# A recurrent attention, a tanh network and an 8-expert layer on one core: order of the first loads, weight conversion through PSUM, a seventh place for weights

## The chip, the cores and the metric

The kernel runs on one core of a Trainium2 chip. The time is that of one execution on the device in microseconds, from three runs of the kernel before: 834.49, 833.47 and 834.39, median 834.39. One more execution was profiled; it took 832.75 us, with a span of 831.2 us from its first to its last instruction. All rows below come from that one.

## The reference, cut to what matters

```python
# r, k, v: [4, 8, 768, 48]; w, u: [8, 48]
def _attn_ref(r, k, v, w, u):
    state = zeros(B, H, D, D)
    for t in range(S):
        kt, vt, rt = k[:, :, t], v[:, :, t], r[:, :, t]
        cur = einsum('bhd,bhe->bhde', u[None] * kt, vt)
        y[:, :, t] = einsum('bhd,bhde->bhe', rt, state + cur)
        state = w[None, :, :, None] * state + einsum('bhd,bhe->bhde', kt, vt)

def _moe_ref(x, w_in, w_out):          # x: [3072, 384], w_in: [384, 2048], w_out: [2048, 384]
    h = x @ w_in
    return (h - np.tanh(h)) @ w_out

def _moe2_ref(x, expert_emb, tau, w1, w2):   # 8 experts, w1: [8, 384, 1024], w2: [8, 1024, 384]
    logits = normalised(x) @ normalised(expert_emb).T / tau
    expert_idx = argmax(logits); gate_w = softmax(logits)[expert_idx]
    out[token] = gate_w * (relu(x @ w1[e]) @ w2[e])      # e = expert_idx of the token

reference = _moe2_ref(_moe_ref(_attn_ref(...)), ...)
```

The arguments `w_in` and `w_out` of the second stage reach the kernel as 64-bit floats. They are read as 64-bit integers, and the kernel makes 32-bit floats of them by shifts and masks of the two 32-bit halves.

## The kernel before, in words

The sequence is cut into 24 tiles of 128 tokens (4 batches by 6 chunks), and three tiles make a block of 384 tokens. There are eight blocks. Every product of matrices is done with numbers split into a high part (type float32r) and a low part, the rest that the high part leaves, with three matmuls for each product (high by high, high by low, low by high).

**Attention of a tile** (class `Att`, L312). `decay_r` and `decay_k` (L324, L327) multiply the transposed r and k of the tile by tables of powers of w. `bonus` (L335, L336) forms r*k*u and `sums` (L340) adds it up over a head, `diagonal` (L348 on ScalarE with eight activations, or L350 on GpSimd with two instructions) makes diagonal matrices of the sums. `scores` (L361) is a TensorE product, `causal` (L366) copies the scores above the diagonal over the diagonal matrix, `values` (L391) multiplies by v and, after the first chunk, by the state, `result` (L396 on ScalarE, L397 on VectorE) writes the high and the low part of xt. `decayed` (L331) and `state_product` (L405), `state_add` (L414, L416, L419) carry the state on.

**Weights.** w_in and w_out come in 16 chunks of 128 x 768 numbers (chunk m: w_in for even m, w_out for odd m), in the order `order` (L1006). A chunk is loaded (L220, L225) into one of six places (`STAGE`, L208), of which two are tiles of their own and four are also the last quarters of the converted weights. `convert` (L228) makes floats of it, in place, with three VectorE instructions over 768 elements: L240 and L243 write `bits`, a tile in SBUF, and L246 writes the place. `split` (L252) then writes the high part on ScalarE (L253) and the low part on GpSimd (L254). A place is free for a later chunk once its chunk is split and, for w_out, transposed for the logits (`Logits`, L256). Logits: the product of w_out with the normalised expert embedding (`embedding_norms`, `embedding_rows`, `embedding_columns`, L1044 to L1060) is put into eight more columns of w_out (L285, L286), so that the second product of the network gives the router's logits as well.

**The network.** For a block, step f of 16 computes 128 hidden columns: `ffn1` (L469, nine matmuls into a PSUM tile ph), `squares` (L516, L517 on ScalarE), `small_tanh` (L525 and L526 on VectorE, L527 and L529 on ScalarE, then glo on VectorE, L532), and, two or three steps later, `ffn2` (L480, nine matmuls into three sums that stay in PSUM). Up to two instructions of a conversion are put between L526 and glo (L530, L531). All PSUM tiles share eight banks (L96).

**The order.** The part from L137 to L1141 is written by hand: within it each engine keeps the program's order (`manual_schedule`, L138). It issues the first loads (L1083 to L1091), the attention of tiles 0, 1 and 2 (block 0), and the first three conversions, in turns. Instructions that come later in the program may be put between those by the planner, which orders all the rest by a model of the time. Then comes a loop (L1194) of 22 steps: six of block 0 and sixteen of block 1, in which the attention of tiles 3, 4 and 5 (`attention_stage`, begun at the steps in `START`, L85) and the other conversions (at the steps in `CONV`, L86) are spread out. After it the other blocks run, each with the attention of the next one, and then the experts, with weights loaded anew. SP issues nearly all loads and stores, one after the other; a load whose buffer isn't free holds back those behind it.

`tc.issue_after(x)` brackets instructions that are to be issued after x; in the kernel before it is used with x on the same engine as the instructions inside it (L710, L746, L824, L1313).

## Time and profile before

| | |
|---|---|
| median of three runs | 834.39 us |
| the profiled execution | 832.75 us |
| its span | 831.2 us |
| TensorE (PE) busy | 773.0 us, 93% of the span |
| VectorE (DVE) busy | 525.6 us, 63% |
| ScalarE (ACT) busy | 440.8 us, 53% |
| GpSimd (POOL) busy | 309.1 us, 37% |
| moved by DMA | 89.69 MB, 108 GB/s over the span |

Shares over the whole span are a mean of stages that differ, so the first 160 us, in which the attention of the first tiles and the conversion of the weights take place, are to be read by themselves: with the busy time of each engine in a stretch, then with the waits of the engine that is due to be the bound, and then with the single instructions of the engine that it waits for. The last number of a waiting row is the longest single wait; "PEclk" is the mean clock that TensorE was granted in a stretch, as a share of 2.4 GHz.

### The profile page before, as it was taken

The numbers are of one execution on the slowest core, as the hardware profiler recorded it, in microseconds if no ns is written. First come the engines' busy times: TensorE is split into PE (matmuls) and PEld (weight loads), VectorE is DVE, ScalarE is ACT, GpSimd is POOL, SyncE is SP. The second block draws the span as 40 slices with busy tenths as digits, with TensorE's granted clock in tenths as the row PEclk, the third lists the DMA queues.
The fourth block names the chain that finished last, engine by engine and source line by source line (L and its number), as shares of the span: only waits on it lengthen the run. The fifth ranks groups of instructions, "written<-read, shape, count | busy, mean of one in ns | idle before, by whom it ended". The sixth has DMA issues, their size and how long they took to land. (4 is left out here: it accounts for less than half of the span.)

```text
span 831.2 us, 15313 instructions
## 1 busy us (share of the span) xinstructions
PE 773.0 (93%) x5835; PEld 726.2 (87%) x5835; DVE 525.6 (63%) x1048; ACT 440.8 (53%) x1007; POOL 309.1 (37%) x312
## 2 busy tenths in 40 slices
PE   6567979999999999999999999999989999999992
PEld 3456968897999999999999999999979999999992
DVE  8999698577786676676676684656554344454510
ACT  1256647555656656656655756777343435454421
POOL 7674254047363173173173250131431214331111
PEclk8578989999999999999999999999999999999996
DMA  8851721024323123123123201050552335544300
GB/s 285 279 162 41 261 71 54 24 84 121 115 69 112 54 85 112 56 82 112 53 85 112 77 8 58 30 181 20 160 165 90 135 113 189 188 132 163 122 28 29
DMA packets 41445, 89.69 MB, mean 108 GB/s; under 512 B 9328, under 2 KB 21024, under 8 KB 40338
## 3 DMA queue, kind: packets, MB, share of 16 engines
q1 hardware_dynamic: 37042, 79.10, 29.2%
q0 software_dynamic: 4320, 9.51, 3.5%
q8 instruction: 48, 0.79, 0.4%
q14 instruction: 35, 0.29, 0.1%
HBM read 69.82 MB, written 19.47 MB: 107 GB/s over the span
## 5 line engine op out<-in xcount | busy, mean ns | idle before, releaser
L469 PE MATMUL ph<-xt,wq 128*128 128x384 f32 (+2 forms) x1712 | 346.6, 345 | 2.6 <-DVE am L366 2.6
L469 PEld LDWEIGHTS ph<-xt,wq 128*128 128x128 f32 x1712 | 307.7, 192 | 7.9 <-DVE am L366 2.7
L480 PE MATMUL acc<-wq,ghi 128*128 128x392 f32 (+2 forms) x1120 | 291.2, 344 | 1.7 <-DVE wq L286 1.7
L480 PEld LDWEIGHTS acc<-wq,ghi 128*128 128x128 f32 (+1 forms) x1120 | 201.0, 188 | 7.4 <-DVE wq L286 2.0
L480 PE MATMUL acc<-wq,glo 128*128 128x392 f32 (+2 forms) x560 | 186.6, 341 | 5.5 <-DVE glo L532 5.5
L480 PEld LDWEIGHTS acc<-wq,glo 128*128 128x128 f32 (+1 forms) x560 | 104.6, 187 | 6.5 <-DVE glo L532 5.8
L516 ACT ACTIVATE z<-ph 128x384 f32<-128x384 f32 x128 | 62.5, 488 | 85.1 <-PE ph L469 84.8
L525 DVE TENSOR_TENSOR ph<-ph,z 128x384 f32<-128x384 f32 x128 | 71.8, 561 | 42.1 <-ACT z L516 41.7
L532 DVE TENSOR_TENSOR glo<-ph,ghi 128x384 fp32r<-128x384 f32 x128 | 70.9, 554 | 43.1 <-ACT ghi L527 42.2
L527 ACT ACTIVATE ghi<-ph 128x384 fp32r<-128x384 f32 x128 | 62.7, 490 | 53.6 <-DVE ph L526 49.2
L701 POOL DMA_INDIRECT out_dram<-ob,gts x27 | 28.7, 1064 | 154.6 <-ACT ob L779 149.1
L517 ACT ACTIVATE q<-z,sb_t 128x384 f32<-128x384 f32 x128 | 78.8, 615 | 3.3
L526 DVE SCALAR_TENSOR_TENSOR ph<-q,ph 128x384 f32<-128x384 f32 x128 | 71.8, 561 | 12.8 <-ACT q L517 4.5
L546 DVE SCALAR_TENSOR_TENSOR glo<-ph,ghi 128x384 fp32r<-128x384 f32 (+2 forms) x56 | 31.5, 563 | 74.1 <-ACT ghi L545 74.1
L529 ACT ACTIVATE mk<-z,lz_t 128x384 bf16<-128x384 f32 x128 | 77.0, 601 | 0.0
L545 ACT ACTIVATE ghi<-ph 128x384 fp32r<-128x384 f32 (+2 forms) x56 | 27.7, 496 | 72.7 <-PE ph L469 72.7
L748 DVE TENSOR_TENSOR wq<-eraw,wq 128x768 fp32r<-128x768 f32 x60 | 55.4, 960 | 16.9 <-ACT wq L747 15.8
L747 ACT ACTIVATE wq<-eraw 128x768 fp32r<-128x768 f32 x64 | 50.5, 837 | 11.5 <-DMA eraw<-in_moe_w_dram 11.5
L335 POOL TENSOR_TENSOR rk<-rkv 128x384 f32<-128x384 f32 x21 | 22.2, 1056 | 89.2 <-ACT xr L566 43.9
L350 POOL TENSOR_TENSOR am<-ident,cd 128x512 f32<-128x512 f32 x42 | 45.0, 1092 | 13.1 <-DVE cd L340 13.0
L254 POOL TENSOR_TENSOR wq<-wraw,wq 128x768 fp32r<-128x768 f32 x16 | 30.6, 1915 | 43.3 <-ACT wq L253 43.3
L327 POOL TENSOR_TENSOR tt<-tt,tab_k 112x512 f32<-112x512 f32 x20 | 36.3, 1815 | 18.9 <-DMA tt<-in_cols_dram 18.9
(272 smaller groups left out, 887.9 us busy)
## 6 DMA issues: line engine op xcount, KB each, us to landing
eraw<-in_moe_w_dram SPq DMA_DIRECT2D x32, 768.0 KB, 4.9
rkv<-in_rows_dram SPq DMA_DIRECT2D x22, 640.0 KB, 5.4
tt<-in_cols_dram SPq DMA_DIRECT2D x22, 448.0 KB, 4.0
xd<-xt SPq DMA_DIRECT2D x8, 1152.0 KB, 6.0
wraw<-in_moe_w_in_dram SPq DMA_DIRECT2D x8, 768.0 KB, 7.4
wraw<-in_moe_w_out_dram SPq DMA_DIRECT2D x8, 768.0 KB, 7.1
xs<-xr SPq DMA_DIRECT2D x21, 192.0 KB, 2.2
first<-in_rows_dram SPq DMA_DIRECT2D x1, 640.0 KB
```

The costliest lines, as they stand in the source:

```text
L350: nc.gpsimd.tensor_tensor(out=a, in0=ident[:, None, :].to_broadcast([P, HP, P]), in1=self.cd[:, :, g:g + 1].to_broadcast([P, HP, P]), op=A ...
L469: nc.tensor.matmul(out=ph, lhsT=lhs[a][:, kk, :], rhs=rhs(b, kk), start=(kk == 0 and p == 0), stop=(kk == nk - 1 and p == 2))
L480: mm = nc.tensor.matmul(out=acc[t], lhsT=g[a][:, t * P:t * P + m], rhs=rhs(b, i), start=(i == span[0] and p == 0), stop=(i == span[1] - 1 ...
L516: nc.scalar.activation(out=z, in_=ph, func=AF.Square)
L517: nc.scalar.activation(out=q, in_=z, func=AF.Square, scale=SS, bias=sb_t)
L525: nc.vector.tensor_tensor(out=ph, in0=ph, in1=z, op=ALU.mult)
L526: nc.vector.scalar_tensor_tensor(out=ph, in0=q, scalar=KC, in1=ph, op0=ALU.add, op1=ALU.mult)
L527: nc.scalar.activation(out=ghi, in_=ph, func=AF.Copy)
L529: nc.scalar.activation(out=mk, in_=z, func=AF.Relu, bias=lz_t, accum_out=zx[:, step:step + 1])
L532: nc.vector.tensor_tensor(out=glo, in0=ph, in1=ghi.bitcast(F32), op=ALU.subtract)
L747: nc.scalar.activation(out=hi[c][:, a], in_=t[:, a], func=AF.Copy)
L748: engs[s % len(engs)].tensor_tensor(out=lo[c][:, a], in0=t[:, a], in1=hi[c][:, a].bitcast(F32), op=ALU.subtract)
```

## The change

Twelve edits, most of them before the loop of 22 steps:

- `convert` works on a chunk in two parts (w_in: two of 384 elements; w_out: 512 and 256). The first two instructions of each part write a PSUM tile from the pool of eight banks instead of `bits` in SBUF, and the third reads it. There are six instructions instead of three for a chunk, and three of them, not two, may stand ahead of glo.
- The space of `bits`, of one of two buffers of `mk` and one of two of `t` gives a seventh place for weights (tag `stg6`), and `STAGE` uses it. `part` and other users of the six places keep theirs.
- First loads: the embedding and tau come ahead of tiles 1 and 2, only three chunks of weights are loaded at the start (`load_next(3)`), the fourth comes after the rows of tile 3, the next after those of tile 4, and tile 5's load comes last of all.
- Hand order: the bonus of tiles 1 and 2 moves from VectorE to GpSimd; the diagonals of tiles 0, 1 and 2 move from GpSimd to ScalarE; tile 2's decays and scores come ahead of the results of tiles 0 and 1; the first conversion, split half by half, comes ahead of tile 2's result, and the second and the third come behind it. The state products of tiles 1 and 0 and the embedding's columns are now in this part.
- `START` and `CONV`: tile 5 begins one step later, and the fourth and the fifth conversion are one step later.
- `store_x` is put in an `issue_after` of the ScalarE instruction L527 of the latest step.

```diff
-    START = (0, 1, 1)
-    CONV = (0, 1, 3, 5, 6, 7, 8, 9, 11, 12, 13, 15, 18)
+    START = (0, 1, 2)
+    CONV = (1, 2, 3, 5, 6, 7, 8, 9, 11, 12, 13, 15, 18)
-    STAGE = (0, 1, 2, 3, 0, 1, 2, 3, 2, 3, 4, 5, 1, 4, 1, 1)
+    STAGE = (0, 1, 2, 3, 6, 0, 1, 2, 3, 6, 4, 5, 1, 6, 1, 6)
-        x = work.tile([P, 2 * DM], I32, name="bits", bufs=1)
+            cuts = [[x.rearrange("p (k f d) -> p f k d", k=NK, d=P)[:, i] for x in (lo, hi)] for i in range(2)]
...
+            cuts = [[x[:, i:j] for x in (lo, hi)] for i, j in ((0, 512), (512, 2 * DM))]
...
+            for l, h in cuts:
+                x = ps.tile([P, 512], I32, tag="p", name="bits")
+                x = x[:, :TOK].rearrange("p (k d) -> p k d", d=P) if win_chunk else x[:, :l.shape[1]]
+                nc.vector.tensor_scalar(out=x, in0=h, scalar1=3, scalar2=0x3FFFFFFF,
+                                        op0=ALU.logical_shift_left, op1=ALU.bitwise_and)
+                yield
+                nc.vector.scalar_tensor_tensor(out=x, in0=l, scalar=29, in1=x,
+                                               op0=ALU.logical_shift_right, op1=ALU.bitwise_or)
+                yield
+                nc.vector.scalar_tensor_tensor(out=l, in0=h, scalar=-0x40000000, in1=x,
+                                               op0=ALU.bitwise_and, op1=ALU.bitwise_or)
+                yield
...
-    def split(f, dst_hi, dst_lo, eng=None):
+    def split(f, dst_hi, dst_lo, eng=None, i=slice(None)):
...
     def store_x(j, xt):
-        nc.sync.dma_start(...)
+        with tc.issue_after(mark["z"]):
+            nc.sync.dma_start(...)
...
-        nc.scalar.activation(out=ghi, in_=ph, func=AF.Copy)
-        mk = work.tile([P, TOK], BF16, name="mk")
+        mark["z"] = nc.scalar.activation(out=ghi, in_=ph, func=AF.Copy).ins
+        mk = work.tile([P, TOK], BF16, name="mk", bufs=1)
...
-        next(between, None)
-        next(between, None)
+        for _ in range(3):
+            next(between, None)
...
-    def load_next():
+    def load_next(n=NF):
-            if before and order[before[-1]] not in done or STAGE[s] > 3 and 5 not in finished:
+            if before and order[before[-1]] not in done or STAGE[s] in (4, 5) and 5 not in finished:
...
+    nc.sync.dma_start(out=en, in_=emb)
+    nc.sync.dma_start(out=tau_t, in_=tau.to_broadcast([P, 1]))
     load_rkv(1)
     load_rkv(2)
-    nc.sync.dma_start(out=en, in_=emb)
-    nc.sync.dma_start(out=tau_t, in_=tau.to_broadcast([P, 1]))
-    load_next()
-    load_rkv(5)
+    load_next(3)
...
     a[0].decay_k(nc.vector)
-    decay_rows()
     a[0].sums()
-    a[0].diagonal()
+    a[0].diagonal(True)
     a[0].scores(range(HP))
+    embedding_norms()
+    a[1].bonus(nc.gpsimd)
     a[1].decay_r(nc.vector)
     a[1].decay_k(nc.vector)
-    a[1].bonus(nc.vector)
     a[1].sums()
+    decay_rows()
+    a[1].diagonal(True)
     a[1].scores(range(HP))
-    a[1].diagonal()
     a[0].causal()
     a[0].values()
-    a[2].bonus(nc.vector)
+    a[2].bonus(nc.gpsimd)
+    a[2].decay_r(nc.vector)
+    a[2].decay_k(nc.vector)
     a[2].sums()
+    a[2].scores(range(HP))
+    a[2].diagonal(True)
     a[1].causal()
     a[1].values()
-    a[2].diagonal()
     a[0].result()
-    a[2].decay_r(nc.vector)
-    a[2].decay_k(nc.vector)
-    a[2].scores(range(HP))
+    a[1].decayed()
+    a[1].state_product()
+    load_rkv(3)
+    load_next(4)
+    a[2].causal()
+    a[2].values()
     a[1].result()
-    embedding_norms()
-    a[1].decayed()
+    ops = convert_next()
+    for i in range(2):
+        for _ in range(3):
+            next(ops)
+        split(*ready[0], i=i)
+    done.add(0)
     a[0].decayed()
+    a[0].state_product()
+    load_rkv(4)
+    load_next()
+    load_rkv(5)
+    a[2].result()
+    embedding_rows()
+    embedding_columns()
     convert_now()
-    a[2].causal()
-    convert_now()
-    split(*ready[0])
-    done.add(0)
-    a[2].values()
-    embedding_rows()
-    a[1].state()
-    a[2].result()
-    load_rkv(3)
-    load_next()
     split(*ready[1])
+    a[2].decayed()
+    a[1].state_add()
     convert_now()
     split(*ready[2])
...
         if i == 0:
-            a[0].state_product()
-            a[2].decayed()
-            load_rkv(4)
-            embedding_columns()
             routing_table()
```

The lines left out give `t` and `mk` one buffer wherever they are made, and name the places.

## Rows read from the trace of the kernel before

**Rows 1.** The page, part 1: busy us (share of the span) xinstructions.

```profile
PE 773.0 (93%) x5835; PEld 726.2 (87%) x5835; DVE 525.6 (63%) x1048; ACT 440.8 (53%) x1007; POOL 309.1 (37%) x312
```

**Rows 2.** Busy time by stretch; columns: start:end, length, engines (instructions), clock, DMA share, GB/s.

```profile
7.70:39.60 31.90, 17.07 (x189) 12.70 (x190) 30.20 (x38) 4.48 (x10) 20.98 (x16) 0.63 0.90 303
39.60:80.00 40.40, 27.08 (x198) 23.23 (x196) 40.21 (x50) 22.86 (x60) 24.08 (x16) 0.75 0.33 105
80.00:110.00 30.00, 30.00 (x316) 27.90 (x316) 22.05 (x36) 19.09 (x47) 10.00 (x6) 0.98 0.67 228
110.00:130.00 20.00, 13.58 (x66) 11.62 (x65) 19.85 (x22) 9.31 (x22) 13.08 (x10) 0.83 0.13 40
```

**Rows 3.** Waits of TensorE, 30 to 130 us: for whom, us, times, longest.

```profile
PE pt L267 <- DVE wraw L246: 8.2, 1, 8.2
PE acc L480 <- DVE glo L532: 5.5, 1, 5.5
PE ps_en L1059 <- DVE en L1054: 4.4, 1, 4.4
PE ph L469 <- DVE am L366: 2.6, 1, 2.6
PE acc L480 <- DVE wq L286: 1.7, 1, 1.7
```

**Rows 4.** Groups of VectorE's instructions, 10 to 82 us: busy us, mean ns.

```profile
L243 DVE SCALAR_TENSOR_TENSOR bits<-wraw,bits 128x768 int32<-128x768 int32 x8 | 15.5, 1936 | 0.0
L246 DVE SCALAR_TENSOR_TENSOR wraw<-wraw,bits 128x768 int32<-128x768 int32 x8 | 9.1, 1135 | 0.1
L240 DVE TENSOR_SCALAR bits<-wraw 128x768 int32<-128x768 int32 x8 | 9.0, 1125 | 0.0
...
L324 DVE TENSOR_TENSOR tt<-tt,tab_r 112x512 f32<-112x512 f32 x4 | 6.9, 1727 | 0.0
...
L336 DVE TENSOR_TENSOR rk<-rk,u_bc 128x384 f32<-128x384 f32 x2 | 1.8, 919 | 0.1
...
L335 DVE TENSOR_TENSOR rk<-first 128x384 f32<-128x384 f32 x1 | 1.4, 1397 | 0.0
...
L335 DVE TENSOR_TENSOR rk<-rkv 128x384 f32<-128x384 f32 x1 | 0.5, 546 | 0.0
```

**Rows 5.** Single lines, to 200 or 300 us: shortest/median/longest ns, first and last start.

```profile
L240 DVE TENSOR_SCALAR bits<-wraw x16: 537/560/2156, 23.7 to 147.2; 128x768 int32<-128x768 int32 x16
L243 DVE SCALAR_TENSOR_TENSOR bits<-wraw,bits x16: 943/1258/7008, 24.3 to 147.8; 128x768 int32<-128x768 int32 x16
L246 DVE SCALAR_TENSOR_TENSOR wraw<-wraw,bits x16: 943/960/2621, 27.5 to 149.2; 128x768 int32<-128x768 int32 x16
L525 DVE TENSOR_TENSOR ph<-ph,z x29: 548/560/567, 49.8 to 196.0; 128x384 f32<-128x384 f32 x29
L366 DVE COPY_PREDICATED am<-cmask,pa x28: 715/727/749, 15.6 to 299.0; 128x512 f32<-128x512 uint8 x28
```

**Rows 6.** Timeline, 111 to 118 us: start us, us, engine, line, operation.

```profile
111.59 7.01 DVE L243 SCALAR_TENSOR_TENSOR bits<-wraw,bits 128x768 int32<-128x768 int32 x1
112.12 1.86 POOL L254 TENSOR_TENSOR wq<-wraw,wq 128x768 fp32r<-128x768 f32 x1
...
116.80 0.99 POOL L336 TENSOR_TENSOR rk<-rk,u_bc 128x384 f32<-128x384 f32 x1
```

**Rows 7.** Timeline at 15 to 56 us, single rows.

```profile
15.75 2.04 POOL L350 TENSOR_TENSOR am<-ident,cd 128x512 f32<-128x512 f32 x2 [1.08 <-DVE cd L340]
...
33.03 0.39 SPq L220 DMA_DIRECT2D wraw<-in_moe_w_in_dram  x1
...
38.62 0.56 DVE L397 TENSOR_TENSOR xt<-py,xt 128x384 fp32r<-128x384 f32 x1
...
55.64 2.44 ACT L348 ACTIVATE am<-ident,cd 128x128 f32<-128x128 f32 x8
```

**Rows 8.** The page, part 6, DMA issues: xcount, KB each, median us to landing.

```profile
wraw<-in_moe_w_out_dram SPq DMA_DIRECT2D x8, 768.0 KB, 7.1
```

More of the change, by code (lines that the diff above doesn't have):

```diff
@@ L206, in rwkv__then__tanh_ffn__then__top1_moe_kernel @@
     CW = 2 * P
-    STAGE = (0, 1, 2, 3, 0, 1, 2, 3, 2, 3, 4, 5, 1, 4, 1, 1)
+    STAGE = (0, 1, 2, 3, 6, 0, 1, 2, 3, 6, 4, 5, 1, 6, 1, 6)
     def stage(i, shape, dt, name):
-        return work.tile(shape, dt, name=name, tag=f"stg{i}" if i < 2 else f"wq{i - 2}3", bufs=1)
+        return work.tile(shape, dt, name=name, tag=f"wq{i - 2}3" if 1 < i < 6 else f"stg{i}", bufs=1)
     def raw(s):
@@ L452, in store_x @@
     def store_x(j, xt):
-        nc.sync.dma_start(out=blocks(xd, j * TOK).rearrange("(p a) d -> p (a d)", p=P),
-                          in_=xt.rearrange("p k i t -> p (k i t)").bitcast(F32))
+        with tc.issue_after(mark["z"]):
+            nc.sync.dma_start(out=blocks(xd, j * TOK).rearrange("(p a) d -> p (a d)", p=P),
+                              in_=xt.rearrange("p k i t -> p (k i t)").bitcast(F32))
     def attention(j):
@@ L486, in tanh_parts @@
         q = work.tile([P, TOK], F32, name="q")
-        t = work.tile([P, TOK], F32, name="t")
-        mk = work.tile([P, TOK], BF16, name="mk")
+        t = work.tile([P, TOK], F32, name="t", bufs=1)
+        mk = work.tile([P, TOK], BF16, name="mk", bufs=1)
         nc.scalar.activation(out=z, in_=ph, func=AF.Square)
@@ L511, in any_tanh @@
         return halves(tanh_join(ph, tanh_parts(ph)))
+    mark = {}
     def squares(ph):
@@ L526, in small_tanh @@
         nc.vector.scalar_tensor_tensor(out=ph, in0=q, scalar=KC, in1=ph, op0=ALU.add, op1=ALU.mult)
-        nc.scalar.activation(out=ghi, in_=ph, func=AF.Copy)
-        mk = work.tile([P, TOK], BF16, name="mk")
+        mark["z"] = nc.scalar.activation(out=ghi, in_=ph, func=AF.Copy).ins
+        mk = work.tile([P, TOK], BF16, name="mk", bufs=1)
         nc.scalar.activation(out=mk, in_=z, func=AF.Relu, bias=lz_t, accum_out=zx[:, step:step + 1])
-        next(between, None)
-        next(between, None)
+        for _ in range(3):
+            next(between, None)
         nc.vector.tensor_tensor(out=glo, in0=ph, in1=ghi.bitcast(F32), op=ALU.subtract)
@@ L568, in finish @@
             nc.sync.dma_start(out=xs[n * P:n * P + P, :DM], in_=xr)
-            junk = work.tile([P, TOK], F32, name="t")
+            junk = work.tile([P, TOK], F32, name="t", bufs=1)
             nc.scalar.activation(out=junk, in_=xr, func=AF.Square, accum_out=ssq[:, t:t + 1])
@@ L831, in narrow @@
     def narrow(jb, slot, alone=False):
-        xt = [work.tile([P, NK, P], F32R, name="xn", tag="q"), work.tile([P, NK, P], F32R, name="xn", tag="t")]
+        xt = [work.tile([P, NK, P], F32R, name="xn", tag="q"), work.tile([P, NK, P], F32R, name="xn", tag="t", bufs=1)]
         columns([slot], xt[0], ((xt[1], 0, NK),), {})
@@ L890, in overflow @@
         g1 = work.tile(shp, F32, name="g1", tag="q")
-        sel = work.tile(shp, F32, name="sel", tag="t")
+        sel = work.tile(shp, F32, name="sel", tag="t", bufs=1)
         jb = jot[:, :, None].to_broadcast(shp)
@@ L984, in gate_row @@
         se = work.tile([P, 1], F32, name="gse", tag="se")
-        junk = work.tile([P, DM], F32, name="gjunk", tag="t")
+        junk = work.tile([P, DM], F32, name="gjunk", tag="t", bufs=1)
         nc.scalar.activation(out=row[:, :DM], in_=acc[:, :DM], func=AF.Copy)
@@ L1044, in embedding_norms @@
     def embedding_norms():
-        en_j = work.tile([E, DM], F32, name="en_j", tag="t")
+        en_j = work.tile([E, DM], F32, name="en_j", tag="t", bufs=1)
         nc.scalar.activation(out=en_j, in_=en, func=AF.Square, accum_out=en_n)
```

15 lines of the change are left out of this document (3 added, 12 removed).

## The prediction

> **What bounds the kernel now.** I read the share of busy time first [rows 1]: TensorE has work for 773.0 of 831.2 us, so at most 58 us can be won by filling its gaps, and some more where its clock was low. The table by stage comes second [rows 2]: TensorE has no gap from 80 to 110 us; its gaps lie before 80 and in 110 to 130. In both of those VectorE is full (40.21 of 40.40 us, 19.85 of 20.00), and so it is in the first stretch (30.20 of 31.90). TensorE's mean granted clock is 0.63, 0.75 and 0.83 in the stretches with gaps and 0.98 in the one without. Third the waits of TensorE from 30 to 130 us [rows 3]: the five longest, 22.4 us together, all end with a VectorE instruction, and the two longest with a conversion of weights (8.2, the first chunk of w_out, which the logit columns need) or with what stood behind one (5.5, glo). So up to 130 us the bound is VectorE's queue, not the amount of TensorE work; after it TensorE is the bound, and what is saved ahead of it stays saved, since the later work is unchanged.
>
> Why is VectorE full? The groups of its instructions [rows 4] and the spread of single durations [rows 5] answer it. The same 128x768 instruction of a conversion, L243, takes 0.943 us at best and 7.008 at worst; L240 0.537 to 2.156; L246 0.943 to 2.621. Instructions that read or write PSUM do not spread: L525 0.548 to 0.567, L366 0.715 to 0.749. The 7.01 us one [rows 6] begins at 111.59, GpSimd runs one tensor_tensor after the other from 112.12 to 117.79, and it ends 0.8 us after the last of these; then glo comes, and TensorE's wait of 5.5 us ends. So what stretches is a VectorE instruction that works from SBUF alone while GpSimd works. All three instructions of a conversion are of that kind; eight of them cost 15.5 + 9.1 + 9.0 = 33.6 us between 10 and 82 us [rows 4], 4.2 each, against 0.54 + 0.94 + 0.94 = 2.4 undisturbed [rows 5].
>
> **The change part by part.** The sum goes against the profiled execution: 832.75 us, its span 831.2, 1.64 (0.2%) under the median of the runs, 834.39.
>
> *Conversions by way of PSUM.* Three instructions of 768 elements become six: two times 384 elements for w_in, 512 and 256 for w_out. Nothing in the trace does an integer operation with a PSUM operand; the nearest rows of equal size are L525 (384, 0.56) and L366 (512, 0.73) [rows 5]. w_in: 6 x 0.56 = 3.4. w_out: by the slope between these two, 256 elements take about 0.39, so 3 x (0.73 + 0.39) = 3.4. Bounds: 2.4 if the halves only share out the undisturbed time, 4.2 if they are stretched as before. I take 3.3, since the two halves can also overlap other short instructions. Eight conversions: 33.6 - 8 x 3.3 = 7.2 us off VectorE (bounds 0 and 14). The trace speaks for a price without spread: no PSUM row has any.
>
> Here a rule of the Trainium skill speaks against the change (VectorE: DVE Perf Modes, Rules for kernel authors): minimise the number of VectorE instructions, as each pays its own drain. By it alone the count doubles and each conversion loses about 0.9 us (3.3 against 2.4), 14 us of VectorE over all 16. The rows agree that there is a fixed share (halving 768 elements takes 0.94 to 0.56, not 0.47), but show it to be less than what waiting costs now.
>
> *Bonus of tiles 1 and 2 from VectorE to GpSimd, diagonals of tiles 0 to 2 from GpSimd to ScalarE.* VectorE loses 1.8 + 1.4 + 0.5 = 3.7 us [rows 4]. GpSimd gains four such instructions of about 1 us and loses three diagonals of 2.04 us [rows 7]; ScalarE takes 2.44 us for a diagonal [rows 7], 7.3 for three. ScalarE is busy for 4.48 of the 31.90 us from 7.7 on [rows 2], so this is beside other work, but each diagonal comes some 0.4 us later, and that of tile 2 now stands ahead of the result of tile 0 in ScalarE's queue, which VectorE and behind it tile 2's masking wait for. I charge 2.5 us of VectorE waiting (0 to 5).
>
> *The hand order.* Before, the third tile's result (L397 at 38.62 [rows 7]) stands on VectorE behind the second conversion; the first product of the feed-forward needs it. After the change it stands behind the first conversion only, and tile 5's decay no longer comes this early (its load goes last). Removed from ahead of it: 3.7 of bonus, one conversion of 4.2, one L324 of 1.7, and 0.9 from the cheaper first conversion: 10.5, so it comes near 28. That moves work, it doesn't remove any: the conversion is due later, so I don't add these 10 us to the sum. What it does give is cover: TensorE has work while conversions 1 and 2 run. The wait for the embedding columns (4.4) and that for the first chunk of w_out (8.2) [rows 3] are then late by less; what is late next is glo behind the conversions, on the same queue.
>
> *Decays (L324) beside GpSimd.* They keep both inputs in SBUF: 6.9 us for four [rows 4], about 1.0 each over the 0.68 of the undisturbed. Bounds: nothing saved, or 4 us; I take 1.5, since GpSimd has 2 us less to do.
>
> *Loads.* Embedding and tau go ahead of tiles 1 and 2: two issues, under 1 us of SP's queue, hidden by tile 0's own work. The fourth chunk of weights, issued with the first three before, now stands on SP behind tile 3's rows, which wait for the state product of tile 1; in the same way the next two stand behind tile 0's. The queue shows this pattern already: the fifth chunk, which waited behind such rows, was issued at 33.03 [rows 7]. By my estimate the fourth is needed near 34 (28, the embedding and two conversions of 3.3) and issued near 24 (when tile 1's state product can run); a landing takes 7.1 [rows 8]: hidden with 3 us to spare. If that cover is gone, conversion 3 waits up to 5 us and glo and the masks wait behind it on VectorE. The seventh place lets the fifth chunk be issued without the first being done, and each later one a conversion sooner: 0 while TensorE is the bound (80 to 110), a reserve elsewhere. Stores of xt (L453), of which one stands just ahead of a load of weights, are put after a ScalarE instruction; before, such a bracket is used for instructions of the same engine (L710), and a store on SP is none, so I count 0 (bounds -1 to 3). One buffer instead of two for mk and t costs nothing: both are mostly written by ScalarE alone, in order.
>
> *A third conversion step ahead of glo.* Three halves (1.7 us) stand there instead of two whole steps (1.5 undisturbed, 3.1 at the means of [rows 4]): counted above.
>
> *110 to 130 us.* The 7.01 us instruction has no counterpart: TensorE's wait of 5.5 goes [rows 3], and with it part of the low clock behind it (0.83 in that stretch); I take 6 of the 6.4 us of idle time there (0 if a decay takes its place, 9 with the clock).
>
> **Sum.** VectorE up to 82 us: 7.2 + 3.7 + 1.5 - 2.5 = 9.9. TensorE's clock there: with fewer gaps some of its instructions run at the higher level; 27.08 us busy at 0.75 [rows 2] would be 20 at full, of which I take 2. Then 6 in 110 to 130. Less 2 for waits on a PSUM bank: the trace has one of 2.6, L469 behind L366 [rows 3], ph waiting for a mask to give its bank back. 9.9 + 2 + 6 - 2 = 15.9, so 832.75 - 15.9 = 816.9, and on the scale of the median 818.5.
>
> **The rivals.**
> (a) *The saving is hidden.* VectorE gets shorter, but the next wait in line (loads behind SP's waits, ScalarE with 7.3 us more) takes the place, and only part of the 22.4 us of TensorE's waits goes: 3 to 8 us saved, 826 to 831. For it: ScalarE and SP get new work ahead of waits. Against it: ScalarE is only 22.86 of 40.40 busy in the second stretch.
> (b) *Banks: slower.* A conversion now takes one of eight PSUM banks twice, for about 1.7 us each, where three are held by sums, two or three by ph, two by a tile's scores. If each of the 13 conversions after the third makes TensorE wait as L469 did for L366 (2.6 us) [rows 3], 34 us are lost; 34 - 18 makes 850. It decides from seven such waits on. For it: that row shows that banks already run out. Against it: only one such wait in 100 us.
> (c) *It doesn't do what it says.* If the halves are stretched by GpSimd as before, or doubling the count weighs more (the skill's rule above), VectorE gains nothing from 8 conversions or loses 7 us; with 3.7 off and 2.5 on, and none of the 6 us later, it comes to 831 to 839. Against it: no stretched PSUM row in [rows 5].
> (d) *More.* VectorE and TensorE both find the full cover of an earlier start: the 10 us of the hand order come on top, 800 to 809.
>
> **How the numbers follow.** Forecast (809 to 826): 0.60. (a) 0.16; (b) 0.11; (c) 0.07; (d) 0.06. The range is from 808 to 831: it takes in the forecast with its bounds (conversions, waits, clock) and (a), and leaves out (b), (c) for the most part, and (d). A difference under 0.2%, 1.7 us, can't be told from none. Faster: 0.60 + 0.16 + 0.06 and a little of (c), 0.83; the same: 0.04, from (c) and the edge of (a); slower: 0.13.
>
> **What would show it.** In the changed trace L243's successors should all lie within a few per cent of 0.56 (w_in); tile 2's L397 should come near 28; VectorE should no longer be full in 110 to 130, and TensorE's waits on VectorE from 30 to 130 should fall from over 20 us to under 10. It is wrong if halves of conversions spread beside GpSimd, if TensorE's waits for ph or scores end with the release of a bank by a conversion, or if VectorE waits for a load of weights in the first 60 us.

## The result, and the profile after

The changed kernel takes 821.15 us (median of four runs, 819.02 to 822.99), beside 834.05 for the kernel before: a ratio of 0.9845, with a 95% interval from 0.9815 to 0.9875. Forecast were 818.5, with a range from 808 to 831. The profiled execution of the changed kernel took 822.99 us, the longest of its four, with a span of 821.3.

Busy time by stretch, as in [rows 2] (start:end, length, then TensorE, its weight loads, VectorE, ScalarE and GpSimd, the clock, DMA share, GB/s):

```profile
7.70:39.60 31.90, 17.02 (x195) 13.95 (x196) 22.70 (x41) 12.93 (x41) 18.41 (x16) 0.68 0.85 293
39.60:80.00 40.40, 34.68 (x294) 29.21 (x292) 33.18 (x68) 24.89 (x62) 20.74 (x15) 0.75 0.50 160
80.00:110.00 30.00, 30.00 (x248) 26.25 (x246) 25.54 (x57) 18.56 (x44) 15.95 (x13) 1.00 0.56 189
110.00:130.00 20.00, 19.95 (x121) 18.83 (x121) 17.20 (x38) 16.36 (x40) 7.61 (x5) 1.00 0.25 80
```

VectorE is no longer full in any of the four (33.18 of 40.40 us where it was 40.21), and TensorE is busy for 34.68 us of the second stretch and 19.95 of the last, where it was 27.08 and 13.58. Its clock in the second stretch did not rise: 0.75 in both kernels.

The waits of TensorE from 30 to 130 us, as in [rows 3]:

```profile
PE pst L410 <- POOL ktok L336: 5.9, 2, 5.5
PE pl L281 <- ACT wt L274: 2.4, 1, 2.4
PE ph L475 <- DVE glo L540: 2.1, 2, 1.8
PE pt L272 <- issue: 1.3, 1, 1.3
PE pt L272 <- DVE wraw L251: 0.5, 1, 0.5
PE ph L475 <- ACT wt L274: 0.3, 1, 0.3
```

The two longest waits of before, 8.2 us for a conversion and 5.5 for glo, have no counterpart; VectorE ends 2.6 us of waiting instead of 22.4. The longest is new: the state product of tile 0 waits 5.5 us for GpSimd's ktok.

The groups of the conversion's three instructions and of a decay (L329) on VectorE, 10 to 82 us, as in [rows 4], and the spread of the first of them over the whole conversion, as in [rows 5]:

```profile
L248 DVE SCALAR_TENSOR_TENSOR bits<-wraw,bits 128x384 int32<-128x384 int32 (+2 forms) x14 | 7.7, 557 | 0.2
L251 DVE SCALAR_TENSOR_TENSOR wraw<-wraw,bits 128x384 int32<-128x384 int32 (+2 forms) x14 | 7.5, 550 | 0.2
L245 DVE TENSOR_SCALAR bits<-wraw 128x384 int32<-128x384 int32 (+2 forms) x14 | 7.5, 554 | 0.1
L329 DVE TENSOR_TENSOR tt<-tt,tab_r 112x512 f32<-112x512 f32 x5 | 4.2, 838 | 1.7 <-DMA tt<-in_cols_dram 1.7
...
L245 DVE TENSOR_SCALAR bits<-wraw x32: 417/551/697, 27.6 to 132.9; 128x384 int32<-128x384 int32 x16, 128x512 int32<-128x512 int32 x8, 128x256 int32<-128x256 int32 x8
```

Fourteen halves are seven conversions: 22.7 us, 3.24 each, where eight cost 33.6, 4.2 each. The shortest and the longest (0.417 and 0.697) are the sizes 256 and 512; no half is stretched any more, though GpSimd is busy for 62.7 us of the four stretches where it was for 68.1 [rows 2]. Of the 48 instructions over 384 elements, the 26 that overlap GpSimd's work took 0.546 to 0.564 us, the other 22 0.535 to 0.561.

### The profile page after: what moved, and what is told of

Read it like the earlier page. It is cut to its first block, busy times and chain, and to the rows that moved or that the text cites. A ratio compares the mean times of both kernels' runs of the same rounds, so it can differ in the third digit from the quotient of the medians.

```text
span 821.3 us, 15368 instructions
## 1 busy us (share of the span) xinstructions
PE 775.1 (94%) x5835; PEld 726.9 (89%) x5835; DVE 512.1 (62%) x1092; ACT 446.6 (54%) x1032; POOL 301.8 (37%) x311
## 5 line engine op out<-in xcount | busy, mean ns | idle before, releaser
L486 PE MATMUL acc<-wq,ghi 128*128 128x392 f32 (+2 forms) x1120 | 288.1, 344 | 0.2 <-ACT ghi L553 0.2
L533 DVE TENSOR_TENSOR ph<-ph,z 128x384 f32<-128x384 f32 x128 | 71.7, 561 | 40.8 <-ACT z L524 40.4
L534 DVE SCALAR_TENSOR_TENSOR ph<-q,ph 128x384 f32<-128x384 f32 x128 | 71.7, 561 | 11.3 <-ACT q L525 2.5
L756 DVE TENSOR_TENSOR wq<-eraw,wq 128x768 fp32r<-128x768 f32 x60 | 55.5, 964 | 18.5 <-ACT wq L755 16.9
L340 POOL TENSOR_TENSOR rk<-rkv 128x384 f32<-128x384 f32 x22 | 22.6, 1026 | 94.0 <-DMA xs<-xr 64.6
L259 POOL TENSOR_TENSOR wq<-wraw,wq 128x768 fp32r<-128x768 f32 (+1 forms) x17 | 30.2, 1774 | 45.2 <-ACT wq L258 45.2
L332 POOL TENSOR_TENSOR tt<-tt,tab_k 112x512 f32<-112x512 f32 x20 | 34.4, 1721 | 26.5 <-DMA tt<-in_cols_dram 21.3
L355 POOL TENSOR_TENSOR am<-ident,cd 128x512 f32<-128x512 f32 x36 | 36.9, 1047 | 10.6 <-DVE cd L345 10.6
```

Of the source, the lines that this page charges most:

```text
L355: nc.gpsimd.tensor_tensor(out=a, in0=ident[:, None, :].to_broadcast([P, HP, P]), in1=self.cd[:, :, g:g + 1].to_broadcast([P, HP, P]), op=A ...
L486: mm = nc.tensor.matmul(out=acc[t], lhsT=g[a][:, t * P:t * P + m], rhs=rhs(b, i), start=(i == span[0] and p == 0), stop=(i == span[1] - 1 ...
L533: nc.vector.tensor_tensor(out=ph, in0=ph, in1=z, op=ALU.mult)
L534: nc.vector.scalar_tensor_tensor(out=ph, in0=q, scalar=KC, in1=ph, op0=ALU.add, op1=ALU.mult)
L756: engs[s % len(engs)].tensor_tensor(out=lo[c][:, a], in0=t[:, a], in1=hi[c][:, a].bitcast(F32), op=ALU.subtract)
```

## Experiments

Each edit was timed beside the kernel before, whose median was 833.99, 835.05 and 837.84 us in the three sets of runs marked A, B and C below; kernels of different sets are therefore compared by their ratios. "Step 24" and "step 160" are the starts of the `ffn1` of these steps (counted through the network's blocks and then the experts, the first is step 0; 160 lies in the experts) in the profiled execution, read in TensorE's timeline.

| kernel | set | median, us | ratio to before, 95% | step 24 | step 160 |
|---|---|---|---|---|---|
| before | | 834.39 | 1 | 170.4 | 710.7 |
| E1 conversion through PSUM alone | A | 814.18 | 0.9753 [0.9726, 0.9779] | 149.0 | 691.3 |
| E2 E1 and work between engines | B | 815.54 | 0.9779 [0.9747, 0.9811] | 150.3 | 693.1 |
| E3 E1 and the seventh place | C | 821.66 | 0.9811 [0.9763, 0.9859] | 151.0 | 697.7 |
| E4 E3 and later steps | C | 823.12 | 0.9829 [0.9778, 0.9879] | 152.7 | 697.9 |
| the changed kernel | | 821.15 | 0.9845 [0.9815, 0.9875] | 155.7 | 700.9 |
| E5 the change, six places | A | 823.23 | 0.9853 [0.9827, 0.9878] | 158.1 | 702.8 |
| E6 E5, halves in SBUF | A | 839.08 | 1.0052 [1.0029, 1.0075] | 173.3 | 718.5 |
| E7 the change, loads early | B | 824.60 | 0.9869 [0.9847, 0.9891] | 161.1 | 704.7 |
| E8 the change, norms late, ktok first | B | 819.89 | 0.9825 [0.9802, 0.9848] | 151.0 | 695.1 |
| E9 the change, columns late | C | 822.97 | 0.9812 [0.9776, 0.9849] | 151.9 | 700.4 |
| E10 E8 and E9 | C | 823.68 | 0.9834 [0.9786, 0.9881] | 154.5 | 702.0 |
| E11 before without GpSimd's splits | B | 823.10 | 0.9848 [0.9823, 0.9872] | 158.0 | 702.1 |

In the expectations, before_psum is E1, psum_seven E3, after_six E5, after_norms_ktok E8 and after_late_columns E9.

The theory at the start was that of the prediction: VectorE instructions that work from SBUF alone are held by GpSimd, and the conversion through PSUM escapes that. The rivals: what is won comes from the new order, or from moving work between engines.

**E1, the conversion alone.** The kernel before with `convert` and the three places ahead of glo as in the change, and nothing else:

```diff
-        x = work.tile([P, 2 * DM], I32, name="bits", bufs=1)
+            for l, h in cuts:
+                x = ps.tile([P, 512], I32, tag="p", name="bits")
...
-        next(between, None)
-        next(between, None)
+        for _ in range(3):
+            next(between, None)
```

> The kernel before with one part of the change alone: conversions in two halves by way of a PSUM bank, and three of their instructions, not two, ahead of glo. Theory (the gain is that conversions are no longer stretched by GpSimd): all halves within 5% of 0.56 or 0.69/0.42 us, TensorE's 5.5 us wait for glo at 113 to 119 gone, 823 to 828 us. Rival (the gain is the hand order, diagonals on ScalarE and bonus on GpSimd): halves may be short, but the start stays as it was and little is won, 831 to 836 us.

It took 814.18 us, 20 under before: this one part brings more than the whole change, and more than the 823 to 828 us expected. Its waits of TensorE, 30 to 130 us, and its stretches:

```profile
PE ph L474 <- DVE xt L402: 5.4, 1, 5.4
PE ph L474 <- DVE am L371: 1.0, 1, 1.0
PE pt L272 <- ACT wt L274: 0.9, 1, 0.9
PE ph L474 <- DVE wraw L251: 0.9, 1, 0.9
...
7.70:39.60 31.90, 17.85 (x171) 13.42 (x172) 30.95 (x51) 4.31 (x9) 21.74 (x18) 0.54 0.88 300
39.60:80.00 40.40, 37.27 (x402) 31.98 (x401) 35.43 (x75) 29.60 (x79) 20.51 (x15) 0.94 0.56 188
80.00:110.00 30.00, 29.17 (x201) 25.97 (x200) 27.88 (x62) 21.77 (x50) 17.72 (x14) 1.00 0.43 146
110.00:130.00 20.00, 20.00 (x126) 18.32 (x125) 14.46 (x32) 14.75 (x36) 4.76 (x3) 1.00 0.24 80
```

No wait for a conversion is over 0.9 us, and waits of ph that end with a mask or a conversion come to 1.9 us in all. From 40 to 80 us TensorE is busy for 37.27 us at a mean clock of 0.94, against 27.08 at 0.75 in [rows 2].

**E2, work moved between engines.** E1 with the bonus of tiles 1 and 2 on GpSimd and three diagonals on ScalarE:

```diff
-    a[0].diagonal()
+    a[0].diagonal(True)
-    a[1].bonus(nc.vector)
+    a[1].bonus(nc.gpsimd)
...
```

> The kernel before_psum (before with conversions by way of PSUM, 814.2 us) with one more part of the change: diagonals of tiles 0 to 2 on ScalarE, bonus of tiles 1 and 2 on GpSimd, in the old order and with the old loads. If this move of work costs part of the 7 us by which the whole change is slower than before_psum (rk from GpSimd comes later than from VectorE, and VectorE waits for it): 817 to 821 us, with waits of VectorE for rk of 2 us and more before 25 us. If it is the order or the loads: 812 to 816. The prediction's own price, 3.7 us off VectorE less 2.5 of waits, would make it 811 to 814.

815.54, not to be told from E1. VectorE's queue got shorter where it had been full, in 7.7 to 27 us from the first of these rows (E1) to the second (E2):

```profile
sum 19.30, PE 12.01 PEld 9.00 DVE 18.60 ACT 2.03 POOL 11.80; mean PE 12.01 PEld 9.00 DVE 18.60 ACT 2.03 POOL 11.80
...
sum 19.30, PE 10.59 PEld 7.97 DVE 13.21 ACT 9.25 POOL 8.92; mean PE 10.59 PEld 7.97 DVE 13.21 ACT 9.25 POOL 8.92
```

VectorE is busy for 5.4 us less there, and yet step 24 comes 1.3 us later and not earlier (150.3 for 149.0). Most of the 5.4 us comes back as waiting for the engines that took over the work, 4.7 us before 27 us, where E1's VectorE waits 0.5:

```profile
DVE cd L345 <- POOL rk L341: 2.9, 2, 2.0
DVE xt L402 <- ACT xt L401: 1.8, 1, 1.8
```

**E5 and E6, PSUM against SBUF in the new order.** E5 is the change with the six places of before; E6 is E5 with the halves in SBUF:

```diff
-    STAGE = (0, 1, 2, 3, 6, 0, 1, 2, 3, 6, 4, 5, 1, 6, 1, 6)
+    STAGE = (0, 1, 2, 3, 0, 1, 2, 3, 2, 3, 4, 5, 1, 4, 1, 1)
...
-                x = ps.tile([P, 512], I32, tag="p", name="bits")
+                x = work.tile([P, 512], I32, name="bits", bufs=1)
```

> The changed kernel with the six places for weights of before (the seventh isn't used). Theory: the seventh place is a reserve only, 820 to 824 us. Rival (loads of weights are what was late): conversions wait for their loads, VectorE idles on DMA for 4 us or more in the first 130 us, 826 us or more.

> The changed kernel with six places, and the two halves of a conversion go by way of a tile in SBUF instead of a PSUM bank (to be compared with after_six; the order, the number of instructions and the sizes are the same). Theory: the halves with two SBUF inputs spread again, the longest over 2 us, and 6 to 12 us of the gain go, 827 to 834 us. Rival (hand order and smaller pieces are the gain): within 2 us of after_six. Banks (rival b of the prediction): faster than after_six, since no bank is taken.

With PSUM 823.23, in SBUF 839.08, slower than before. VectorE's groups by form, 10 to 82 us, in E6:

```profile
L251 DVE SCALAR_TENSOR_TENSOR wraw<-wraw,bits 128x384 int32<-128x384 int32 x8 | 7.6, 945 | 0.1
L248 DVE SCALAR_TENSOR_TENSOR bits<-wraw,bits 128x384 int32<-128x384 int32 x8 | 6.0, 754 | 0.2
L245 DVE TENSOR_SCALAR bits<-wraw 128x384 int32<-128x384 int32 x8 | 4.4, 547 | 0.2
...
L329 DVE TENSOR_TENSOR cols<-cols,tab_r 112x512 f32<-112x512 f32 x1 | 4.2, 4153 | 0.0
```

The second and the third instruction of a half, which have two inputs, take 0.754 and 0.945 us where those with a PSUM operand take 0.55; the first, with one input, is as fast as there (0.547). So the operand's place decides, not the halving: with the same count, sizes and order it is worth 16 us (839.1 to 823.2), more than the 6 to 12 expected. In the old order, halving, PSUM and the third step ahead of glo together are worth 20 (834.0 to 814.2); the third step was not tried by itself. With PSUM in both, the rest of the change (but for the seventh place) costs 9 us (814.2 to 823.2). That is where the question moved: what in the rest loses?

**E11, without GpSimd's share.** To show that GpSimd is what stretches, the kernel before without GpSimd's sixteen splits: ScalarE writes zeros for the low parts of the weights, sixteen instructions more, and the result leaves these parts out:

```diff
-        (eng or nc.gpsimd).tensor_tensor(out=dst_lo, in0=f, in1=dst_hi.bitcast(F32), op=ALU.subtract)
+        nc.scalar.activation(out=dst_lo, in_=f, func=AF.Copy, scale=0.0)
```

> The kernel before, where the low part of each converted chunk is written as zeros by ScalarE instead of by GpSimd's subtraction, so the low parts of w_in and w_out are left out of the result; GpSimd loses 16 instructions of 1.88 us, ScalarE gains 16 of 0.9 us. Theory (GpSimd's work is what stretches the conversions from SBUF): the mean of L243 from 10 to 82 us falls from 1.94 to 1.5 or less, the three instructions together from 4.2 to 3.4 or less, 822 to 831 us in spite of ScalarE's new work. Rival (DMA or ScalarE stretches them): spread as before, 834 to 842 us.

```profile
L243 DVE SCALAR_TENSOR_TENSOR bits<-wraw,bits 128x768 int32<-128x768 int32 x9 | 11.0, 1217 | 0.1
L246 DVE SCALAR_TENSOR_TENSOR wraw<-wraw,bits 128x768 int32<-128x768 int32 x9 | 9.9, 1100 | 0.1
L240 DVE TENSOR_SCALAR bits<-wraw 128x768 int32<-128x768 int32 x9 | 7.8, 872 | 0.7 <-DMA wraw<-in_moe_w_in_dram 0.6
```

The same three instructions over 768 elements, untouched, cost 3.19 us a conversion instead of 4.2 [rows 4], L243 1.217 instead of 1.936, and the time falls by 1.5%. GpSimd's work is a cause, not only a neighbour in time. Attention's GpSimd instructions remain, and so does some of the stretch. The trace of before says the same of the rivals DMA and ScalarE: its 15 instructions of L243 and L246 (of 32) that no GpSimd instruction overlaps took 0.943 to 0.960 us, the 17 others 0.946 to 7.008.

A first try at this had a copy of the number itself in place of the low part:

> The kernel before, where the low part of each converted chunk is written by a ScalarE copy of the number itself instead of GpSimd's subtraction: the low part is not the rest that it should be, and GpSimd loses 16 instructions of 1.88 us while ScalarE gains 16 of 0.9 us. Theory (GpSimd's work is what stretches the conversions): the mean of L243 from 10 to 82 us falls from 1.94 to 1.4 or less, the three instructions of a conversion from 4.2 to 3.4 or less, and 3 to 8 us are won in spite of ScalarE's new work, 826 to 831 us. Rival (DMA or ScalarE stretches them): spread as before, 834 to 840 us.

It took 6131 us, and its time says nothing on the question: the router sends the tokens elsewhere, and TensorE waits 1315.5 us for rows of the experts' tokens. Its first 82 us, ahead of the router's effect, agree with E11: the three instructions cost 3.24 us a conversion. A kernel with a data-dependent part must be cut where the data stays plausible.

**E7, loads early.** The prediction saw the late fourth chunk as the risk of the new order. The change with that load and tile 5's at the start:

```diff
-    load_next(3)
+    load_next(4)
+    load_rkv(5)
...
-    load_next(4)
...
-    load_rkv(5)
```

> The changed kernel, with the load of the fourth chunk and of tile 5 back at the start, ahead of everything that waits (the embedding stays early, the seventh place stays). Theory L (the late loads cost: VectorE waited 2.9 us for cols and 1.7 for tt after 24 us, and tiles 3 to 5 came late): those two waits go and 4 us or more are won, 814 to 818 us. Theory O (the hand order costs): 819 to 823, as the change.

824.60: no gain, and TensorE waits longer in the same place (30 to 130 us):

```profile
PE pst L410 <- POOL ktok L336: 16.1, 2, 12.3
```

With tile 5's data there early, the planner puts more of the bonus and the decays (L340, L332) on GpSimd ahead of tile 0's ktok, which comes at 40.59 us instead of 32.94. One of them waits for tile 3's columns:

```profile
32.26 1.71 POOL L332 TENSOR_TENSOR tt<-tt,tab_k 112x512 f32<-112x512 f32 x1 [5.37 <-DMA tt<-in_cols_dram]
```

Their load is now issued at 19.93 us (14.45 in the changed kernel), behind the loads that were put first. So one late load was exchanged for another; this edit doesn't win anything as the rest of the order stands, and it doesn't show that late loads cost nothing.

**E8, norms late, ktok first.** The change with the embedding's norms where its rows are made, and tile 0's `decayed` (ktok) ahead of the first conversion:

```diff
-    embedding_norms()
...
+    a[0].decayed()
     ops = convert_next()
...
-    a[0].decayed()
...
+    embedding_norms()
     embedding_rows()
```

> The changed kernel with two steps of its hand order moved: the norms of the embedding come just ahead of its rows instead of between tiles 0 and 1, and the ktok of tile 0 (GpSimd) comes ahead of the first conversion instead of behind its split. Theory O (the order costs): VectorE's wait of 3.0 us for ScalarE's en_j at 11 to 14 us and TensorE's 5.5 us for ktok at 28 to 34 us go, the first product of the network comes 3 us earlier or more, 815 to 818 us. Theory L (late loads): 819 to 823.

819.89; by the ratios (0.9825 and 0.9845, intervals that overlap) it isn't settled that this is faster, nor which of the two theories holds, though step 24 starts 4.7 us earlier. The wait was exchanged for another:

```profile
PE ps_en L1067 <- DVE en L1062: 10.1, 1, 10.1
PE pst L410 <- POOL ktok L336: 1.7, 1, 1.7
```

**E9 and E10, state product and columns behind the first product.** In the changed kernel, tile 0's state product and the embedding's columns stand ahead of the network's first `ffn1` in TensorE's queue; in before they stand behind it:

```diff
-    a[0].state_product()
-    load_rkv(4)
...
-    embedding_columns()
...
         if i == 0:
+            a[0].state_product()
+            load_rkv(4)
+            embedding_columns()
             routing_table()
```

> The changed kernel with one piece of its hand order as before: the state product of tile 0, the load of tile 4 behind it and the embedding's columns stand again behind the first ffn1 of step 0, not ahead of it. Theory Q: these TensorE instructions, which wait for ktok from GpSimd (5.5 us) and for the embedding's rows, hold back the network's first product and with it all that follows; taking them out of the way wins back most of the 7 us by which the changed kernel stands behind the conversion alone: 814 to 818, and TensorE's wait for ktok ahead of its first ffn1 is gone. Rival W: these products wait for what GpSimd and VectorE do and not for their place, and the wait turns up elsewhere (py, ph or pt): 820 to 825, as the changed kernel.

> The edit of after_late_columns and that of after_norms_ktok together: norms of the embedding late, ktok of tile 0 made ahead of the first conversion, and the state product, the load and the columns behind the first ffn1. In after_norms_ktok the late norms made TensorE wait 10.1 us for the columns ahead of the first ffn1; behind it that wait has cover. Theory Q: 812 to 817, the least of the versions with the new hand order. Rival W: 818 to 823.

As ratios 0.9812 and 0.9834: both under 0.9845, but the intervals overlap, E9's only just touches E1's, and E10's lies above that. In E9 the wait for ktok is gone (5.9 to 0.5) and step 24 starts 3.8 us earlier; in E10 the same edit on top of E8 puts it 3.5 later than E8. As a ratio, Q asked for 0.976 to 0.981 from E9 and W for 0.983 to 0.989, so E9 decides nothing; E10's 0.9834 lies where W put it (0.981 to 0.987), though its interval reaches into Q's 0.974 to 0.980. So theory Q isn't borne out as the one explanation: the place of these two products is part of the loss at best. TensorE waits for tile 2's result instead (xt L401, 3.1 us in E9, 7.3 in E10).

**E3 and E4, the seventh place and the later steps.** E1 with `STAGE` and the single buffers of t and mk, and that with `START` and `CONV`:

```diff
-    STAGE = (0, 1, 2, 3, 0, 1, 2, 3, 2, 3, 4, 5, 1, 4, 1, 1)
+    STAGE = (0, 1, 2, 3, 6, 0, 1, 2, 3, 6, 4, 5, 1, 6, 1, 6)
...
-    START = (0, 1, 1)
-    CONV = (0, 1, 3, 5, 6, 7, 8, 9, 11, 12, 13, 15, 18)
+    START = (0, 1, 2)
+    CONV = (1, 2, 3, 5, 6, 7, 8, 9, 11, 12, 13, 15, 18)
```

> The kernel before with the conversion by way of PSUM and the seventh place for weights, and nothing else of the change. If the seventh place is worth the 2 us that it seemed to be worth in the changed kernel (823.2 against 821.2), 811 to 813.5; if it is a reserve that nothing uses, as the prediction counted, 813.5 to 815.5, as the conversion alone (814.2).

> psum_seven with the later steps of the change for tile 5 and the fourth and the fifth conversion (START, CONV). What is left between it and the changed kernel is the order of the loads and the hand order alone. If those two carry the loss, this one stays at 812 to 815.5; if the later steps carry it, 818 to 822.

By ratio E3 loses 0.6% on E1 (the intervals just overlap, 0.9763 and 0.9779), where a gain or nothing was expected, and E4 0.2% more, which is within the intervals. Two places of these traces can be followed.

The first is between steps 2 and 4, where all versions with the later steps are slow. The time from the `ffn1` of step 2 to that of step 4, and how long TensorE ran at the lower of its two levels (1.2 GHz) in the last such stretch before 70 us:

| | E1 | E2 | E3 | E4 | the change | E5 | E7 | E8 | E9 | E10 |
|---|---|---|---|---|---|---|---|---|---|---|
| step 2 to step 4, us | 13.6 | 13.2 | 13.5 | 18.2 | 18.5 | 18.0 | 18.2 | 16.0 | 16.8 | 18.0 |
| at the lower level, some us | 3 | 3 | 3 | 14 | 17 | 17 | 14 | 3 | 7 | 3 |

E3 and E4 differ by `START` and `CONV` alone: 4.7 us more for these two steps, and 10 more at the lower level. E10 has the long steps without the long low stretch (18.0 us, 3 us), so the clock isn't the whole of it. TensorE in 50 to 60 us, in the order E1, E4, the changed kernel, E9:

```profile
50.00:60.00 10.00, 9.02 (x87) 7.84 (x86) 8.62 (x17) 8.19 (x25) 5.88 (x4) 0.94 0.48 158
...
50.00:60.00 10.00, 9.97 (x39) 8.79 (x39) 9.96 (x21) 7.45 (x19) 3.90 (x4) 0.50 0.38 120
...
50.00:60.00 10.00, 8.06 (x32) 6.87 (x32) 9.92 (x20) 5.83 (x15) 7.50 (x6) 0.50 0.37 126
...
50.00:60.00 10.00, 8.00 (x43) 7.11 (x44) 9.94 (x21) 6.91 (x19) 7.02 (x7) 0.83 0.57 192
```

E4 has hardly a gap (9.97 of 10.00) and is slow all the same, at 0.50; by the busy time alone it would pass for the best of the four. E4 reaches step 2 ahead of E3 by 2.5 us (49.2 for 51.7) and step 4 behind it by 2.1. By step 26 E4 is ahead again (164.9 for 165.4).

The second place is step 26: E3 is 2.0 us behind E1 at step 24 and 5.0 there (165.4 for 160.4). TensorE, VectorE and GpSimd in E3 around 160 us:

```profile
164.00 0.19 PE L589 MATMUL pk<-oh,tri 128*128 128x8 bf16 x1 [2.83 <-DVE oh L586]
...
159.86 2.98 DVE L580 TENSOR_TENSOR l<-l,mx 128x24 f32<-128x24 f32 x1
...
159.09 1.79 POOL L332 TENSOR_TENSOR tt<-tt,tab_k 112x512 f32<-112x512 f32 x1 [1.86 <-DMA tt<-in_cols_dram]
160.85 0.99 POOL L336 TENSOR_TENSOR ktok<-rkv,ktab 128x384 f32<-128x384 f32 x1
161.80 0.99 POOL L340 TENSOR_TENSOR rk<-rkv 128x384 f32<-128x384 f32 x1
```

and the same two engines in E1:

```profile
157.21 1.06 DVE L580 TENSOR_TENSOR l<-l,mx 128x24 f32<-128x24 f32 x1
...
156.44 1.79 POOL L332 TENSOR_TENSOR tt<-tt,tab_k 112x512 f32<-112x512 f32 x1 [1.22 <-DMA tt<-in_cols_dram]
158.76 1.02 POOL L336 TENSOR_TENSOR ktok<-rkv,ktab 128x384 f32<-128x384 f32 x1 [0.53 <-DMA rkv<-in_rows_dram]
```

L580, a step of the router over 24 elements, works from SBUF and starts in both while GpSimd multiplies. In E1, GpSimd has a gap at 158.23, and L580 ends 0.04 us later. In E3, three instructions of GpSimd follow each other without a gap until 162.79, and L580 ends 0.05 us after the last. The median of its eight in E3 is 0.185 us. TensorE's count for the routing waits 2.83 us for it. It has the signs of the conversion's stretch, in an instruction whose size doesn't matter; whether it cost 1 or 3 us hung in these two cases on whether GpSimd's next data was there yet.

GpSimd doesn't keep its turn each time. In the kernel before, a conversion's L243 began while GpSimd split another chunk, and GpSimd's next instructions followed without a gap:

```profile
56.48 2.17 POOL L254 TENSOR_TENSOR wq<-wraw,wq 128x768 fp32r<-128x768 f32 x1
58.61 3.41 POOL L336 TENSOR_TENSOR rk<-rk,u_bc 128x384 f32<-128x384 f32 x2
...
57.32 2.14 DVE L243 SCALAR_TENSOR_TENSOR bits<-wraw,bits 128x768 int32<-128x768 int32 x1
```

L243 ended 0.81 us after the split, and the two L336 took 3.41 us, where one takes 1.02 in the median: here GpSimd was the one that waited. What decides between the two was not settled.

## Why the prediction was right, and where it wasn't

The time lies 2.7 us above the forecast and well inside the range. The mechanism of the conversions was right, and it carries the gain; that the total came out so close is luck. The conversion alone won 20 us where its terms in the sum were 13, and all the rest, taken at 2.7 us won (3.7 and 1.5, less 2.5), lost some 7. The sum against the stretches: busy time times mean clock, an estimate of the work of TensorE at full clock, from 7.7 to 130 us:

| | 7.7 to 39.6 | 39.6 to 80 | 80 to 110 | 110 to 130 | sum | ahead of before | at step 24 |
|---|---|---|---|---|---|---|---|
| before [rows 2] | 10.8 | 20.3 | 29.4 | 11.3 | 71.7 | | |
| the changed kernel | 11.6 | 26.0 | 30.0 | 20.0 | 87.5 | 15.8 | 14.7 |
| E1 | 9.6 | 35.0 | 29.2 | 20.0 | 93.8 | 22.1 | 21.4 |

The mean clock of a stretch counts its idle time too; weighted by the clock of the busy time alone, the two leads come to 16.8 and 23.6.

- *The sum up to 130 us: right in size, by luck.* 15.9 were predicted; 15.8 by the estimate, and 14.7 by the start of step 24. TensorE's busy time up to 110 us rose by 7.6 us (9.9 predicted from VectorE); in 110 to 130 it rose by 6.4 (6 predicted); what is left for the clock is 1.9 (2 predicted). For waits on a bank 2 were charged; of TensorE's new waits only 0.5 us end with a conversion. Each of these figures is what the conversion won less what the rest lost, so that they meet the terms doesn't make the terms right.
- *The bound: VectorE's queue, right for the later stretches only.* Up to 39.6 us VectorE is busy for 7.5 us less than before (22.70 for 30.20), and TensorE's busy time there is the same (17.02 for 17.07). In E2, too, VectorE's shorter queue gave TensorE nothing.
- *The price of a conversion: right.* 3.24 us for 3.3, w_in halves 0.55 for 0.56, w_out 0.69 and 0.42 for 0.73 and 0.39. The rule that I weighed, the Trainium skill's "VectorE: DVE Perf Modes", Rules for kernel authors (minimise the count of instructions), would have made the change lose; E1 doubles the count and wins 20 us, and E5 and E6 keep the count, change only the place, and differ by 16. Another page of the Trainium skill, "SBUF — State Buffer", Who interferes with whom, says that a VectorE instruction with at most one SBUF input, outside its two-port modes, doesn't contend with GpSimd. The halves by way of PSUM (0.417 to 0.697, by size) agree with that.
- *What it is worth: wrong.* E1 shows 20 us from the conversion alone, where its terms in the sum (7.2, 6, the clock's 2, less 2 for banks) were 13. Two steps failed. One is that a microsecond off VectorE gives one to TensorE: eight conversions cost 7.1 us less in E1 (26.5 for 33.6), as predicted, but TensorE's busy time up to 80 us rose by 11.0. The other is the clock: I took 2 us of "27.08 us busy at 0.75"; in E1 the second stretch is at 0.94. Its busy time in the four stretches is 16.6 us over before's (104.3 for 87.7), so by this estimate 5.5 of the 22.1 are the clock. The 2 us for banks were not seen.
- *The hand order, with the rest of the change: wrong.* I counted it as 0, at best a gain of 10 (rival d). E1 against the changed kernel says that all the rest of the change loses: 6.7 us by step 24, and 0.9% by the ratios, whose intervals don't meet. Which part loses is not settled. In the profiled executions that add its parts one by one, step 24 falls behind by 2.0 (seventh place and single buffers), 1.7 (later steps) and 3.0 (moves, hand order, loads), step 160 by 6.4, 0.2 and 3.0; by the ratios the parts are 0.6%, 0.2% and 0.2%, none clear of the intervals. The cover came: tile 2's result stands at 32.02 us (38.62 before [rows 7], near 28 predicted), and step 1 starts at 40.7 us, 2.7 ahead of before and 1.5 ahead of E1. It was lost between 44 and 70 us:

```profile
48.44 1.50 PE L281 MATMUL pl<-wt,ent 128*32 128x128 f32 x12 [2.38 <-ACT wt L274]
51.69 3.25 PE L475 MATMUL ph<-xt,wq 128*128 128x384 f32 x9 [1.76 <-DVE glo L540]
...
47.82 0.69 DVE L329 TENSOR_TENSOR cols<-cols,tab_r 112x512 f32<-112x512 f32 x1 [2.87 <-DMA cols<-in_cols_dram]
48.43 0.56 DVE L533 TENSOR_TENSOR ph<-ph,z 128x384 f32<-128x384 f32 x1
```

  Step 1's product is done by 44 us. Then TensorE has gaps for ScalarE's wt (2.38 us, from 46.06) and for glo (1.76); its clock falls at 47.6 us, within the first of them, and stays low to 64.7. VectorE, for its part, stands for 2.87 us ahead of a decay whose columns, tile 5's, are now loaded last; the tanh of step 0 (L533) and with it glo stand behind that. It is the wait on a load in the first 60 us that the prediction named as what would make it wrong, for other data than the weights it had in mind. E7 takes this wait away, and gets one for tile 3's columns and the longer one for ktok.
- *Bonus and diagonals: wrong.* 3.7 off and 2.5 of waiting were to leave 1.2 won. E2 shows no gain: 5.4 us off VectorE and 4.7 of waiting. VectorE waits for GpSimd and ScalarE in the changed kernel as well (3.02 us before 14.09 for the norms, 2.53 before 17.96 for the bonus), which is rival (a) for this part.
- *Decays beside GpSimd: too small.* 1.5 were taken; the mean of the `tt` decays fell from 1.73 us [rows 4] to 0.84, 3.6 us for four, near the bound of 4.
- *Loads: right for the weights, wrong for tile 5.* The fourth chunk is issued at 25.83 us (near 24 predicted), and VectorE doesn't wait for it. The load of tile 5, which I had only as a decay less on VectorE, is the 2.87 us above.
- *The seventh place and single buffers: 0 predicted.* Six places in the change are 2.1 us slower in the median (E5; intervals overlap); in the old order the place and the single buffers together seem to lose 0.6% (E3; intervals just overlap). Neither sign is shown. Single buffers of t and mk, which I also put at nothing, are in both of E5 and E3: not tried by themselves, they are an open rival for what E3 loses.
- *The bracket around the store: 0, right.* Without it every engine has the same instructions in the same order, so it was not timed by itself.
- *"What is saved ahead stays saved": wrong by 5 us.* The lead of 14.7 us at step 26 is 13.8 at step 40, 10.5 at step 128 and 9.9 at step 160. L580 beside GpSimd shows one way in which 3 us go in the planner's blocks (E3); in the changed kernel TensorE waits 2.9 us for masks from 160 to 640 us, 1.1 in E1. The rest was not settled, and the profiled execution was the longest of its four runs.
- *Banks, rival (b): not seen.* Waits of ph that end with a mask or a conversion come to 1.9 us in E1, and those that end with a conversion to 2.7 in E3, where 34 were feared.

Still open: why the lower level lasts 3 us in one order and 17 in another. E8, E9 and E10 shorten it without the median following beyond its interval. The lowest median here is that of E1, 814.18 us, 0.9753 of before, and some 0.9% under the changed kernel by the two ratios; E2 can't be told from it.

## What to carry to other kernels

When one kind of instruction has a wide spread, look at what the other engine does during its longest cases, and change the place of its operand before its count or its order: one operand in PSUM was worth 16 us with all else alike, the conversion as a whole 20, and the rest of this change together lost some of it. A term that shortens the gaps of TensorE should be priced with the clock of the stretch behind the gaps, at both levels. A change with many edits wants its largest one run alone; the total here was right to 0.3%, by luck, with terms that were not.

## What the runs showed of the hardware

A VectorE instruction that reads two operands from SBUF and starts beside GpSimd's work can be held over several instructions of GpSimd, not only the one that runs: 2.98 us for 24 elements over three that followed each other, 0.185 in the median. In another case it got through behind the first of them, and GpSimd's next two took 3.41 us for 2. An integer instruction over strided 32-bit halves with an operand in PSUM took 0.42, 0.55 and 0.69 us for 256, 384 and 512 elements, the same whatever GpSimd did. And a busy TensorE can be a slow one for long: nine matmuls of a step took 3.25 us at 51.69 in the changed kernel and 1.81 at 42.24 in E1 (the second at full clock). The changed kernel's clock fell in a gap of 2.38 us and stayed at the lower level for 17 us, and E4 ran 9.97 of 10.00 us busy at 0.50.
